# One burst of TensorE for a unit's y and the next unit's C.B and B^T x, with decays made in place

## Chip, cores, metric

The kernel runs on one core of a Trainium2 chip. The metric is device time in microseconds (us) of one execution. Engines are named as the profile names them: PE (TensorE), PEld (its weight loads), DVE (VectorE), ACT (ScalarE), POOL (GpSimd), SP (SyncE).

## The reference

```python
# x (4,8,768,32), a, B, C: 4 batches, 8 heads, 768 tokens, head 32, state 16
for c in range(seq // 32):                      # Mamba2 scan, by chunk
    cum = np.cumsum(log(clip(a)), -1)           # decays
    M = einsum(C, B) * causal(exp(cum_i - cum_j))
    y = einsum(M, x) + einsum(C, state) * exp(cum)
    state = exp(sum) * state + sum(B x * exp(cum_last - cum))
# then, for all 3072 tokens of width 256, in fp32
h = y @ w_in;  g = h * sigmoid(h);  out = g @ w_out      # 256 -> 2048 -> 256
```

## The kernel before

It works in 12 units of 256 tokens (four chunks of 64 tokens each). The scan of later units is slipped between the full matmuls of the two-layer part, which fill PE. One pair of units is one stage of eight slots; a slot is 14 full matmuls of 0.432 us (two passes each), 6.04 us. For each unit PE gets two bursts of small tiles. The first burst needs `BT`, a product that GpSimd makes of B and the decays:

```python
def f_B(u, engine=nc.gpsimd):
    BT[u] = sc.tile([128, 2, H, N], FP32, name="BT")
    engine.tensor_tensor(out=BT[u], in0=bn[u], in1=E[u][:, :, :, Q-1:Q]..., op=ALU.mult)

def f_G(u):
    f_D0(u)      # B^T x: 32 (24) tiles of 64 rows x 32 columns, needs BT[u]
    f_G0(u)      # C.B:   32 tiles of 32 x 64

def f_Y(u):      # [cut]
    # state part: 32 (24) tiles of 32 x 64, then
    # y inside the chunks: 64 tiles of 64 x 32, accumulated over it

def scan_plan(G):                      # [cut] which slot each piece stands in
    plan[j + 1][0].extend([E1[2], E1[3], partial(f_B, u), partial(f_C, u)])
    plan[j + 1][2].append(partial(f_G, u))
    ...
    plan[j + 2][2].append(partial(f_Y, u))
```

A plan's lists are emitted between the slot's seven matmul groups. GpSimd also adds output pieces (`p_add`, 128x256, four in a row in some slots). GpSimd runs its instructions in the order in which they were emitted.

## Time and profile before

| | before |
|---|---|
| median of 3 runs | 351.63 us (351.53 to 351.83) |
| profiled span | 350.1 us |
| PE busy | 343.5 us (98%) |
| granted clock, mean | 1.00 |

The prediction below shows the rows that carry the argument.

The timeline of POOL shows where BT stood: right at the start of its slot, 2.3 us ahead of the burst at 198.50, with a length of 0.64 us (columns: start, length, engine, line, operation, operands, idle time before).

```profile
196.20 0.64 POOL L340 TENSOR_TENSOR BT<-bn,E 128x256 f32<-128x256 f32 x1 [2.74 <-DVE E L303]
```

VectorE's timeline at the four additions of 203.73, which the prediction shows, has a pair of additions from SBUF (TN) beside the last of them:

```profile
206.20 1.82 DVE L534 TENSOR_TENSOR TN<-gT 128x512 f32<-128x512 f32 x2
```

And the chain of waits around unit 4's y (L458 and L467), with full matmuls in front of it and behind it and no hole:

```profile
91.68 1.73 PE hp L495 x8
93.41 0.62 PE gy L458 x32
94.03 0.79 PE gy L467 x53
94.82 1.92 PE o_ps L631 x8
```

### The profile page before, as it was taken

Reading aid. Unit: us, or ns where it says so; the run is one execution under the profiler, and the core shown is the slowest. Engines: PE = TensorE matmul, PEld = TensorE weight load, DVE = VectorE, ACT = ScalarE, POOL = GpSimd, SP = SyncE. Lnnn points to the kernel's source line nnn. Section 1 sums busy time; section 2 is a strip of 40 time slices with the busy share of each in tenths; the row PEclk is TensorE's granted clock in tenths of the full one; section 3 lists DMA queues with packets and bytes.
Section 4 is the critical chain, followed back from the end, with each engine's and each line's share of the span. In section 5 each row is a group of like instructions: output and inputs, shape, how many; then the busy total and the mean of one; then the engine's idle time right before and its main releaser. Section 6 shows DMA issues by size and latency. Waiting matters only on the chain.

```text
span 350.1 us, 8358 instructions
## 1 busy us (share of the span) xinstructions
PE 343.5 (98%) x3307; PEld 287.6 (82%) x3308; DVE 205.7 (59%) x408; ACT 162.3 (46%) x396; POOL 112.4 (32%) x140
## 2 busy tenths in 40 slices
PE   8989999999999999999999999999999999999996
PEld 3668888888888888888888888888888888888884
DVE  7998979976795764544663563664652231234812
ACT  2577585323323545355645454644545454454100
POOL 4445335443185032244042244042234112041200
PEclk9999999999999999999999999999999999999999
DMA  6978987799766789965179955057404237512202
GB/s 114 221 239 201 259 279 141 123 214 205 141 123 120 130 171 166 160 122 85 20 160 168 175 100 105 16 106 144 86 2 75 51 56 143 99 38 42 42 2 46
DMA packets 117376, 42.79 MB, mean 122 GB/s; under 512 B 102488, under 2 KB 109144, under 8 KB 117336
## 3 DMA queue, kind: packets, MB, share of 16 engines
q1 hardware_dynamic: 110328, 25.67, 34.9%
q0 software_dynamic: 4464, 16.25, 24.9%
q10 hardware_dynamic: 2544, 0.33, 0.6%
q8 instruction: 26, 0.43, 0.5%
q14 instruction: 14, 0.11, 0.1%
HBM read 22.83 MB, written 3.15 MB: 74 GB/s over the span
## 4 chain that ended last, share of the span: by engine, by line
PE 91%; DVE 4%; DMA 2%; issue 1%; SPq 0%; ACTq 0%; POOL 0%; ACT 0%; DVEq 0%
PE o_ps L631 36%; PE hp L686 28%; PE hp L495 15%; PE hp L631 3%; PE gy L467 2%; PE o_ps L617 2%; PE gy L404 2%; PE gy L458 2%; DMA gT<-in_a_dram 1%; PE gy L389 1%; DVE wv L178 1%; DVE E L415 1%; DMA tbc<-in_B_dram 1%; DVE st L430 0%; DMA out_dram<-ot 0%
## 5 line engine op out<-in xcount | busy, mean ns | idle before, releaser
L689 DVE TENSOR_TENSOR gT<-hp,p 128x256 f32<-128x256 f32 x64 | 26.9, 420 | 73.8 <-ACT p L700 37.8
L495 PE MATMUL hp<-XM,w_in_sb 128*128 128x256 f32 x256 | 59.4, 382 | 1.1 <-POOL w_in_sb L182 0.9
L631 PE MATMUL o_ps<-gT,w_out_sb 128*128 128x256 f32 x240 | 60.4, 379 | 0.0
L692 ACT ACTIVATE gT<-gT 128x256 f32<-128x256 f32 x96 | 39.7, 414 | 43.8 <-DVE gT L689 43.8
L495 PEld LDWEIGHTS hp<-XM,w_in_sb 128*128 128x128 f32 x256 | 47.8, 190 | 9.2 <-POOL w_in_sb L182 2.0
L686 PE MATMUL hp<-raw 128*128 128x256 f32 x192 | 52.7, 380 | 0.0
L548 POOL TENSOR_TENSOR ps<-ps 128x256 f32<-128x256 f32 x35 | 29.3, 838 | 71.4 <-ACT ps L578 70.1
L631 PEld LDWEIGHTS o_ps<-gT,w_out_sb 128*128 128x128 f32 x240 | 45.4, 190 | 6.3
L543 POOL DMA_DIRECT2D gT<-gT x31 | 27.2, 907 | 65.8 <-PE hp L686 22.9
L686 PEld LDWEIGHTS hp<-raw 128*128 128x128 f32 x192 | 36.2, 190 | 5.4 <-POOL ps L548 0.6
L700 ACT ACTIVATE p<-hp 128x256 f32<-128x256 f32 x64 | 24.6, 384 | 27.4 <-PE hp L686 25.9
L689 DVE TENSOR_TENSOR gT<-hp,u 128x256 f32<-128x256 f32 x32 | 13.6, 424 | 38.8 <-PE hp L686 38.8
L686 PE MATMUL hp<-XM,w_in_sb 128*128 128x256 f32 x128 | 34.1, 389 | 0.0
L497 ACT ACTIVATE gT<-hp 128x512 f32<-128x512 f32 x32 | 18.9, 595 | 27.3 <-PE hp L495 27.3
L686 PEld LDWEIGHTS hp<-XM,w_in_sb 128*128 128x128 f32 x128 | 23.3, 190 | 4.3 <-issue 1.0
L303 DVE TENSOR_TENSOR_SCAN E<-ab,diag 128x256 f32<-128x256 f32 (+1 forms) x32 | 25.3, 832 | 0.4
L578 ACT ACTIVATE ps<-o_ps 128x256 f32<-128x256 f32 x38 | 14.5, 383 | 23.9 <-PE o_ps L631 21.0
L340 POOL TENSOR_TENSOR BT<-bn,E 128x256 f32<-128x256 f32 x12 | 9.4, 782 | 47.8 <-DVE E L303 39.6
L631 PE MATMUL o_ps<-gT,wu 128*128 128x256 f32 x88 | 22.4, 380 | 0.0
L631 PE MATMUL o_ps<-gT,wv 128*128 128x256 f32 x88 | 22.2, 380 | 0.0
L631 PE MATMUL o_ps<-gT,raw 128*128 128x256 f32 x80 | 20.5, 380 | 0.0
L686 PE MATMUL hp<-raw,w_in_sb 128*128 128x256 f32 x64 | 19.1, 380 | 0.0
(125 smaller groups left out, 520.8 us busy)
## 6 DMA issues: line engine op xcount, KB each, us to landing
gT<-gT POOLq DMA_DIRECT2D x31, 512.0 KB, 6.1
ab<-in_a_dram SPq DMA_DIRECT2D x40, 128.0 KB, 3.2
raw<-in_moe_w_in_dram SPq DMA_DIRECT2D x8, 512.0 KB, 5.6
raw<-in_moe_w_out_dram SPq DMA_DIRECT2D x8, 512.0 KB, 6.0
xt<-in_x_dram SPq DMA_DIRECT2D x24, 128.0 KB, 5.3
out_dram<-ot SPq DMA_DIRECT2D x92, 32.0 KB, 1.7
bn<-in_B_dram SPq DMA_DIRECT2D x22, 64.0 KB, 2.4
tbc<-in_C_dram SPq DMA_DIRECT2D x40, 32.0 KB, 4.8
```

Source lines behind the costliest of these rows:

```text
L303: nc.vector.tensor_tensor_scan(out=E[u].rearrange("p k h t -> p (k h t)")[:, Q * g0:Q * (g0 + n)], data0=t.rearrange("p g t -> p (g t)"), ...
L340: engine.tensor_tensor(out=BT[u], in0=bn[u], in1=E[u][:, :, :, Q - 1:Q].to_broadcast([128, 2, H, N]), op=ALU.mult)
L495: nc.tensor.matmul(out=hp[:, i], lhsT=w_in_sb[:, kc, f * 128:(f + 1) * 128], rhs=xm[:, kc], start=(kc == 0), stop=(kc == KC - 1))
L497: nc.scalar.activation(GTS[g][:, :, j], hp, AF.Silu)
L543: nc.gpsimd.dma_start(out=o[:, js], in_=a[:, js], accum_op=ALU.add)
L548: engine.tensor_tensor(out=o, in0=p, in1=q, op=op)
L578: nc.scalar.activation(pn, on, AF.Copy)
L631: nc.tensor.matmul(out=o, lhsT=w(j), rhs=g()[:, j], start=(j == 0), stop=(j == last))
L686: nc.tensor.matmul(out=o, lhsT=w, rhs=x_, start=start, stop=True, skip_group_check=True)
L689: nc.vector.tensor_tensor(out=o, in0=p, in1=q, op=ALU.add)
L692: nc.scalar.activation(o, i, AF.Silu)
L700: nc.scalar.activation(o, i, AF.Copy)
```

## The change

The intent: PE pays for every change of tile mode (in the trace of the kernel before, 0.093 us behind a full pass and about 0.092 at the other changes), so y of unit u, C.B and B^T x of unit u+1 are put into one burst for u = 4 and 6 to 10; the state part of y becomes 16 (12) wide tiles. To have the next unit's decays in time they are made earlier, over their own input. The diff, cut to its core:

```diff
-    loads2 = ...(tc.tile_pool(name="loads2", bufs=2))
+    loads2 = ...(tc.tile_pool(name="loads2", bufs=3))
-            E[u] = sc.tile([128, 2, H, Q], FP32, name="E")
+            E[u] = ab[u] if u in ab else loads2.tile([128, 2, H, Q], FP32, name="ab")
+    gy = ps_s.tile([128, 4, 512], FP32, name="gy")     # one PSUM tile for all units
+    def f_Y0w(u):                                      # wide state part
+        ...
+                nc.tensor.matmul(out=yp[:, 2*w+c, 64*k:64*k+64], lhsT=sp[64*w:64*w+64, t],
+                                 rhs=cw[64*w:64*w+64, Q*t:Q*t+Q], start=False, stop=True, ...)
+    def f_YG(u):
+        f_G0(u + 1)
+        f_D0(u + 1)
+        f_Y1(u, True)
+        f_Y0w(u)
     [cut: scan_plan is rewritten]
+        decays(c, 3, 4, 4, 5)      # the last part, with f_B(c), stands in slot 5
+        burst(b, 5)                # f_YG(b), at the end of slot 5
```

More of the change, by code (lines that the diff above doesn't have):

```diff
@@ L59 @@
     loads = ctx.enter_context(tc.tile_pool(name="loads", bufs=3))
-    loads2 = ctx.enter_context(tc.tile_pool(name="loads2", bufs=2))
+    loads2 = ctx.enter_context(tc.tile_pool(name="loads2", bufs=3))
     rawp = ctx.enter_context(tc.tile_pool(name="rawp", bufs=7))
@@ L84, in load_pa @@
         b, t0 = at(u)
-        pa[u] = loads.tile([128, UT], FP32, name="pa")
+        pa[u] = sc2.tile([128, UT], FP32, name="pa")
         q.dma_start(out=pa[u], in_=bass.AP(tensor=a.tensor, offset=a.offset + b * H * S + t0,
@@ L263 @@
         nc.vector.tensor_reduce(out=par[:, e:e + 1], in_=hm[:, e::2], op=ALU.add, axis=AX.X)
+    par4 = const.tile([128, 4], FP32, name="par4")
+    nc.gpsimd.tensor_tensor(out=par4, in0=hm[:, 0:4], in1=hm[:, 4:8], op=ALU.add)
     pz = const.tile([128, 4, Q + 1], FP32, name="pz")
@@ L270 @@
             nc.gpsimd.memset(t[:, :, 0:1], n)
-    E, M, BT, BH, CT, CE, CW, PFX, ST, SM, DP, XM, GTS, BX = ({} for _ in range(14))
+    E, M, BT, BH, CT, CE, CW, PFX, ST, SM, XM, GTS, BX = ({} for _ in range(13))
+    gy = ps_s.tile([128, 4, 512], FP32, name="gy")
+    yp = gy[:, :, 384:512]
     def f_P01():
@@ L382, in f_D0 @@
         else:
-            DP[u] = ps_s.tile([128, 4, 512], FP32, name="gy")
-            d = [DP[u][:, c, 256:384] for c in range(2)]
+            d = [gy[:, c, 256:384] for c in range(2)]
         d = [o.rearrange("p (k x) -> p k x", k=2) for o in d]
@@ L397, in f_G0 @@
         bh, ce = BH.pop(u), CE[u]
-        if u not in DP:
-            DP[u] = ps_s.tile([128, 4, 512], FP32, name="gy")
         for k in range(2):
@@ L403, in f_G0 @@
                 for g in range(4):
-                    nc.tensor.matmul(out=DP[u][64 * c:64 * c + 64, g, 128 * k:128 * k + 128],
+                    nc.tensor.matmul(out=gy[64 * c:64 * c + 64, g, 128 * k:128 * k + 128],
                                      lhsT=bh[32 * g:32 * g + 32, ts], rhs=ce[32 * g:32 * g + 32, :, ts],
@@ L414, in f_M @@
         M[u] = m = E[u].rearrange("p k (g e) t -> p k g (e t)", e=2)
-        nc.vector.tensor_tensor(out=m[:, k], in0=DP[u][:, :, 128 * k:128 * k + 128], in1=m[:, k], op=ALU.mult)
+        nc.vector.tensor_tensor(out=m[:, k], in0=gy[:, :, 128 * k:128 * k + 128], in1=m[:, k], op=ALU.mult)
     def f_S(u, t0=0, t1=4):
@@ L431, in f_S, with f_SM, f_GMD, f_SMD @@
                                                in1=BX[u][c][:, k], op0=ALU.mult, op1=ALU.add)
-    def f_SM(u):
+    def f_SM(u, wide=False):
         t0 = 1 if u % UPB == 0 else 0
-        SM[u] = sc.tile([128, 4, 64], FP32, name="sm")
-        for e in range(2):
-            nc.scalar.activation(SM[u][:, t0:, 32 * e:32 * e + 32], ST[u][:, t0:, 32 * e:32 * e + 32],
-                                 AF.Copy, scale=par[:, e:e + 1])
-    def f_GMD(u):
+        SM[u] = sc.tile([128, 4, 128], FP32, name="sm")
+        for e in range(4 if wide else 2):
+            nc.scalar.activation(SM[u][:, t0:, 32 * e:32 * e + 32], ST[u][:, t0:, 32 * (e % 2):32 * (e % 2) + 32],
+                                 AF.Copy, scale=(par4 if wide else par)[:, e:e + 1])
+    def f_GMD(u, wide=False):
         f_G(u)
+        f_SMD(u, wide)
+    def f_SMD(u, wide=False):
         f_S(u)
-        f_SM(u)
+        f_SM(u, wide)
         for k in range(2):
             f_M(u, k)
-    def f_Y(u):
+    def f_Y0(u):
         first = u % UPB == 0
-        sp, cw, m, xc = SM.pop(u), CW.pop(u), M.pop(u), xt.pop(u)
-        m = m.rearrange("p k g (e t) -> p k (g e) t", e=2)
-        y = ps_s.tile([128, 4, 512], FP32, name="gy")
+        sp, cw = SM.pop(u), CW.pop(u)
         for t in range(1 if first else 0, 4):
@@ L457, in f_Y, with f_Y1 @@
                 w, q = divmod(g, 2)
-                nc.tensor.matmul(out=y[64 * q:64 * q + 64, 2 * w + c, 64 * k:64 * k + 64],
-                                 lhsT=sp[32 * g:32 * g + 32, t], rhs=cw[32 * g:32 * g + 32, Q * t:Q * t + Q],
+                nc.tensor.matmul(out=yp[64 * q:64 * q + 64, 2 * w + c, 64 * k:64 * k + 64],
+                                 lhsT=sp[32 * g:32 * g + 32, t, :64], rhs=cw[32 * g:32 * g + 32, Q * t:Q * t + Q],
                                  start=(k == 0 or (first and t == 2)), stop=False,
                                  tile_position=(32 * g, 64 * q), skip_group_check=True)
+    def f_Y0w(u):
+        sp, cw = SM.pop(u), CW.pop(u)
+        for t in range(1 if u % UPB == 0 else 0, 4):
+            k, c = divmod(t, 2)
+            for w in range(2):
+                nc.tensor.matmul(out=yp[:, 2 * w + c, 64 * k:64 * k + 64], lhsT=sp[64 * w:64 * w + 64, t],
+                                 rhs=cw[64 * w:64 * w + 64, Q * t:Q * t + Q], start=False, stop=True,
+                                 tile_position=(64 * w, 0), skip_group_check=True)
+    def f_Y1(u, start):
+        m, xc = M.pop(u), xt.pop(u)
+        m = m.rearrange("p k g (e t) -> p k (g e) t", e=2)
         for k in range(2):
@@ L466, in f_Y @@
                         h = 4 * w + q
-                        nc.tensor.matmul(out=y[32 * q:32 * q + 32, 2 * w + c, 64 * k:64 * k + 64],
+                        nc.tensor.matmul(out=yp[32 * q:32 * q + 32, 2 * w + c, 64 * k:64 * k + 64],
                                          lhsT=xc[64 * c:64 * c + 64, k, h], rhs=m[64 * c:64 * c + 64, k, h],
-                                         start=False, stop=True, tile_position=(64 * c, 32 * q),
+                                         start=start and k == 0, stop=not start, tile_position=(64 * c, 32 * q),
                                          skip_group_check=True)
-        DP[u] = y
+    def f_Y(u):
+        f_Y0(u)
+        f_Y1(u, False)
+    def f_YG(u):
[3 more added lines that the diff above has]
+        f_Y0w(u)
     def f_X(u):
         XM[u] = xmp.tile([128, 4, 128], FP32, name="XM")
-        y = DP.pop(u)
         n = 2 if u < 2 else 4
         for i in range(0, 4, n):
-            nc.scalar.activation(XM[u][:, i:i + n], y[:, i:i + n, 0:128], AF.Copy)
+            nc.scalar.activation(XM[u][:, i:i + n], yp[:, i:i + n], AF.Copy)
     def new_g():
@@ L713, in f_x1 @@
                 add(g0[:, 0, j], W, p1)
-                other(dve, 2 if j in (2, 5) else 0)
+                other(dve, 2 if len(dve) > 5 else 0)
             elif what == "5":
@@ L768, in scan_piece @@
             elif what == "G":
-                f_GMD(u)
+                f_GMD(u, u == 4)
+            elif what == "J":
+                f_YG(u - 1)
+                f_X(u - 1)
+                f_C(u)
+                f_SMD(u)
             elif what == "Y":
@@ L776, in scan_plan @@
         plan = [([], [], []) for _ in range(8)]
-        for i in range(2):
-            u, j = 2 * G + i, 3 * i
-            E0 = [partial(f_E0, u, q, 2) for q in range(2)]
-            E1 = [partial(f_E1, u, q, 4) for q in range(4)]
-            plan[j][0].extend([partial(f_P0, u), partial(f_P1, u), E0[0], E0[1], E1[0], E1[1]])
-            plan[j][1].extend([partial(f_T2, u, 0), partial(f_T2, u, 1)])
-            plan[j + 1][0].extend([E1[2], E1[3], partial(f_B, u), partial(f_C, u)])
-            plan[j + 1][2].append(partial(f_G, u))
-            plan[j + 2][0].extend([partial(f_S, u, 0, 2), partial(f_S, u, 2, 4), partial(f_M, u, 0),
-                                   partial(f_M, u, 1)])
-            plan[j + 2][1].append(partial(f_SM, u))
-            plan[j + 2][2].append(partial(f_Y, u))
-            plan[j + 3][1].append(partial(f_X, u))
-            if u + 1 < NU:
-                plan[(2, 7)[i]][0].extend([partial(f_T, u + 1, 0), partial(f_T, u + 1, 1)])
+        a, b, c = 2 * G, 2 * G + 1, 2 * G + 2
@@ new lines, in states, with decays @@
+        def states(u, j):
+            plan[j][0].extend([partial(f_C, u), partial(f_S, u, 0, 2), partial(f_S, u, 2, 4), partial(f_M, u, 0),
+                               partial(f_M, u, 1)])
+            plan[j + 1][1].append(partial(f_SM, u, u + 1 < NU))
+        def decays(u, *js):
+            todo = ([partial(f_P0, u), partial(f_P1, u), *(partial(f_E0, u, q, 2) for q in range(2))],
+                    [partial(f_E1, u, q, 4) for q in range(2)], [partial(f_T, u, i) for i in range(2)],
+                    [partial(f_E1, u, q, 4) for q in range(2, 4)] + [partial(f_B, u)])
+            for j, part in zip(js, todo):
+                if 0 <= j < 8:
+                    plan[j][0].extend(part)
+            if js[3] < 8:
+                plan[js[3]][1].extend([partial(f_T2, u, 0), partial(f_T2, u, 1)])
@@ new lines, in burst @@
+        def burst(u, j):
+            plan[j][2].append(partial(f_YG if u + 1 < NU else f_Y, u))
+            plan[j + 1][1].append(partial(f_X, u))
+        if G == 3:
+            plan[0][0].extend([partial(f_E1, a, 2, 4), partial(f_E1, a, 3, 4), partial(f_B, a)])
+            plan[0][1].extend([partial(f_T2, a, 0), partial(f_T2, a, 1)])
+            plan[0][2].append(partial(f_G, a))
+            states(a, 1)
+            decays(b, 1, 1, 2, 2)
+            burst(a, 2)
+            states(b, 3)
+            decays(c, 4, 4, 5, 5)
+        else:
+            decays(b, -1, 0, 0, 1)
+            burst(a, 1)
+            states(b, 2)
+            if c < NU:
+                decays(c, 3, 4, 4, 5)
@@ L792, in scan_plan @@
+        burst(b, 5)
+        if c < NU:
+            states(c, 6)
+            decays(c + 1, 7, 8, 8, 9)
         return plan
@@ L905 @@
             f_s2(2)
-        scan_piece(4, j, ("TE", "DCS", "G", "YS", "", "", "", ""))
-        scan_piece(5, j, ("", "", "T", "E", "DCS", "G", "YS", ""))
+        scan_piece(4, j, ("TE", "DCS", "G", "S", "", "", "", ""))
+        scan_piece(5, j, ("", "", "T", "E", "DS", "J", "YS", ""))
         scan_piece(6, j, ("",) * 7 + ("t",))
@@ L911 @@
                 f_XT(2, i)
+            f_P(6)
+            for q in range(2):
+                f_E0(6, q, 2)
+            for q in range(2):
+                f_E1(6, q, 4)
         f_s2((4, 4, 4, 4, 4, 2, 0, 4)[j])
@@ L920 @@
             f_TS(1, 3, 0)
-        if j in (2, 5):
-            load_unit(6 + j // 3)
+        if j in (2, 5, 7):
+            load_unit({2: 6, 5: 7, 7: 8}[j])
+    NEXT = {(2, 2): 9, (2, 5): 10, (3, 1): 11}
     for G in range(2, NU // 2):
@@ L944 @@
                     f_XT(G + 1, i)
-            if j in (2, 5) and 2 * G + 4 + j // 3 < NU:
-                load_unit(2 * G + 4 + j // 3)
+            if (G, j) in NEXT:
+                load_unit(NEXT[G, j])
     P = NU // 2 - 1
```

## The prediction

Four readings of the kernel before (timeline of PE and PEld, 177 to 187 us) belong beside the text. What it calls a drain is the gap that the records show at a change of mode: the last full pass starts at 177.278 and the first small one at 177.588, which is 0.093 us more than the usual 0.216. Its 0.054 us for 64 columns is a quarter of that 0.216; waves of B^T x, which have 64 columns, start 0.055 us apart there. Where it takes 0.107 us for 128 columns, of a pass or of a load, the trace shows 0.109 for both. That some passes of y go slower than others is measured (0.238 and 0.376 us for 32 each); why is not shown, and that y goes at the slower rate behind 32 other pairs was my estimate.

> **What bounds the kernel now.** I read the page first: busy shares, the forty slices, the chain that ended last.
>
> ```profile
> PE 343.5 (98%) x3307; PEld 287.6 (82%) x3308; DVE 205.7 (59%) x408; ACT 162.3 (46%) x396; POOL 112.4 (32%) x140
> ...
> PE   8989999999999999999999999999999999999996
> ...
> DVE  7998979976795764544663563664652231234812
> ...
> PE 91%; DVE 4%; DMA 2%; issue 1%; SPq 0%; ACTq 0%; POOL 0%; ACT 0%; DVEq 0%
> ```
>
> TensorE (PE) is full from slice 5 to the last but one, and 91% of the chain is PE. A busy PE need not be at its peak, so I next read the chain of waits in order of time over one stage. Its columns are start, length, what:
>
> ```profile
> 177.23 0.43 PE o_ps L631 x2
> 177.66 0.36 PE gy L389 x24
> 178.01 0.62 PE gy L404 x32
> 178.64 1.06 PE hp L686 x4
> 179.70 0.86 PE o_ps L631 x4
> ...
> 184.45 0.43 PE o_ps L631 x2
> 184.88 0.62 PE gy L458 x32
> 185.50 0.79 PE gy L467 x53
> 186.29 1.06 PE hp L686 x4
> 187.35 1.29 PE o_ps L631 x6
> ```
>
> A full 128x128 matmul of 256 columns takes 0.216 us (0.86 for four), one after the other, without a hole. L389 is B^T x, L404 is C.B, L458 and L467 are the two halves of y: small tiles that stand between the full ones. So each unit of the scan costs PE two bursts. B^T x with C.B costs 178.64 - 177.66 = 0.98 us, plus 1.06 - 0.86 = 0.20 for the slow first full matmul behind it: 1.18 us (24 passes of B^T x; 1.20 with 32). y costs 186.29 - 184.88 + 0.20 = 1.61 us (1.49 where the first part has 24 passes). Everything else here runs beside PE. A change is worth what it takes from these bursts, less any wait that it puts in front of PE.
>
> [...] By the start of each pass in the records, the first small pass comes 0.093 us late behind a full one, and B^T x to C.B, the two halves of y, and the way back each show about 0.092 us beyond the columns still streaming (0.054 us for 64 columns, 0.107 for 128). [...] behind a drain two full loads start 0.109 us apart, and the first wave of a mode loses 0.104 us with 128 columns of weights, 0.050 with 64, 0.025 with 32. [...] in y's second part the first 32 passes go in 0.238 us, the next 32 take 0.376.
>
> **The change, part by part.** (a) C.B and B^T x of unit u+1 now stand with y of unit u in one burst, for u = 4, 6, 7, 8, 9, 10: six merged bursts, with 4's and 6's C.B and 5's and 11's y still alone. (b) In the merged burst the order is C.B, B^T x, the intra-chunk part of y, then the state part, which becomes 8 matmuls of 64 rows x 128 columns (16 passes, or 12) in place of 32 (24) of 32x64. (c) The scan E is written over its own input; decays start about four slots earlier. (d) ScalarE makes four masked state slices instead of two. (e) The order of PSUM and buffers follows.
>
> Cost of a merged burst from the durations above: entry 0.093; C.B 0.425 from first to last start; to B^T x 0.197; B^T x 0.238; the y part has the same 64x32 mode, so no drain, but it now comes behind 32 pairs[...], so I charge it all at the slower rate: 0.67; to the state part 0.146; the state part; way back 0.146 + 0.104. The state part decides. It has 64 moving columns (0.054 us), but each load has 128 columns (0.107 us). Two row tiles run side by side, so 8 waves x 0.107 = 0.856 us, against 0.477 for the 32 narrow passes before[...]. With 12 passes it is 0.64.
> Sum, 32 and 16 passes: 0.093 + 0.425 + 0.197 + 0.238 + 0.67 + 0.146 + 0.856 + 0.250 = 2.88 us. With 24 passes of B^T x 2.81[...]. With 32 and 12, 2.66.
> Before: the same pairs cost 1.18 + 1.61 = 2.79, 1.20 + 1.61 = 2.81 and 1.20 + 1.49 = 2.69.
> Six bursts after: 3 x 2.81 + 2.88 + 2 x 2.66 = 16.63 us. Before: 3 x 2.79 + 2.81 + 2 x 2.69 = 16.56. So what is saved by two fewer mode changes (about 0.3 us each burst) goes back into wide weight loads. Net about 0[...].
>
> New waits. A merged burst needs the next unit's BT (POOL, L340) about 0.7 us after it starts. At slot 5 of the first two scan stages that plan for units 8 and 10, the built order puts BT on POOL behind four additions of the outputs. Where those stand, timeline of POOL:
>
> ```profile
> 203.73 3.15 POOL L548 TENSOR_TENSOR ps<-ps 128x256 f32<-128x256 f32 x4 [6.25 <-ACT ps L578]
> ```
>
> The slot's matmuls begin at 199.61 and end 14 x 0.432 = 6.04 us later. The additions end at 206.88, slot + 7.27; BT takes 0.64, so it is ready at slot + 7.9 and a semaphore later. B^T x wants it at 6.04 + 0.093 + 0.425 + 0.197 = 6.76. PE waits 1.18 us, twice: 2.4 us. Before, BT stood in slot 4, where POOL had only its buffer copies ahead: at 196.19 it ran 2.3 us ahead of the burst at 198.5.
> In the stage that plans unit 7, VectorE gets eleven items in one slot: states 1.1, masks 2 x 0.64, prefix 0.98, clipping 1.0, two scans 1.26, besides three additions of 0.42. That is about 6.9 us for a slot of 6.04, and TN's 0.65 behind it, so an addition that a following matmul accumulates over comes about 0.3 us late; I take 0.4 us in all.
> Sum: 0.07 + 2.36 + 0.4 = 2.8 us[...]: +2.4.
>
> (c) by itself wins nothing: in the waits of the kernel before, PE waits for no scan from 45 us on, and at the start the scan of unit 1 stands on VectorE behind the weights' bit work (the chain has L178 at 15.23, then L303 at 16.45), not behind y. (d) adds 2 x 0.31 us of ScalarE per unit, which is busy about half of the time.
>
> **Rivals.**
> 1. The wide loads are hidden and the state part streams at 0.055 us per wave: 8 x 0.055 = 0.44 instead of 0.86. Then each burst saves 0.42 more, 2.4 us over six (12 passes save less), and the total is 351.7 with the waits, or about 349 without. For it: the narrow loads do overlap matmuls. Against it: they overlap one load per matmul, and here the load is the longer of the two.
> 2. The two row tiles do not load side by side: 16 x 0.107 = 1.7 us, +0.86 a burst, +4.6 us in all: about 358.5. Against it: before, four row tiles load in one wave of 0.058 us.
> 3. No wait for BT, because the drain and C.B in front cover it: 351.5 and below. Against: the POOL sum above misses by over a microsecond.
> 4. VectorE becomes the bound in the crowded slots and PE waits in each: 357 or more. Its row in the forty slices shows 4 to 7 tenths there, so only the one stage is at risk.
>
> **Range and chances.** Predicted 354.0 us (351.63 + 2.4). Low end 350.8: rival 1 with most of the waits[...]. High end 356.6: waits in three bursts and costlier decays. 2% is 7.0 us, more than all twenty bursts of units 2 to 11 could give by halving mode changes, so faster by 2% has 0.02; slower by 2% needs rival 2 or 4 with the waits: 0.05; within 2%: 0.93.
>
> **What would show each step.** The time from the last full matmul before a merged burst to the second after it: 2.7 to 2.9 us where there is no wait. The starts of the 16 wide passes: pairs 0.107 us apart (mine), 0.055 (rival 1), or singly 0.107 (rival 2). The 64 passes of y: 0.67 us or about 0.45. In the waits, a PE load of B^T x waiting for POOL BT, twice, 1.0 to 1.3 us each, in slot 5 before the bursts that hold units 8's and 10's B^T x; if it is absent, the step on POOL's order is wrong. In the stage of units 6 and 7, PE waits for VectorE's additions of some tenths. The last stage without scan (281.5 to 321.8 us before) should keep its 40.3 us. I am wrong if merged bursts cost 2.4 us or less with no wait in front, or if the state part is slower than loads side by side allow.

## More of the kernel before

The clock row, granted clock in tenths for 40 slices, says that PE was never slowed:

```profile
PEclk9999999999999999999999999999999999999999
```

## The result

The changed kernel takes 365.33 us (363.39 to 366.22, six runs) against 351.64 (351.48 to 352.05, six runs of the kernel before). The ratio is 1.0384, with an interval of 1.0357 to 1.041: slower by 3.8%, outside the predicted range of 350.8 to 356.6. All ratios here are the mean time of one kernel's fast runs over that of the other's of the same rounds, so they are not quite the ratio of the medians. All runs count as fast except where said.

The page of the changed kernel: span, busy times, the PE and clock rows, and the shares of the chain that ended last.

```profile
span 363.2 us, 8181 instructions
...
PE 348.5 (96%) x3219; PEld 293.7 (81%) x3220; DVE 209.6 (58%) x408; ACT 165.5 (46%) x408; POOL 114.4 (31%) x141
...
PE   7989999999899999979999979999999999999996
...
PEclk9999999999999999969999998999999999999999
...
PE 85%; DVE 5%; POOL 2%; issue 2%; DMA 2%; ACT 1%; SPq 0%; ACTq 0%; DVEq 0%; POOLq 0%
```

PE has 88 instructions fewer and is still busy 5.0 us longer. Busy time that grows with less work points to a slower clock, and the clock row has two dents, in slices 18 and 25. PE's row has a 7 in slice 18 and one in slice 24, just before the second dent. The waits of PE name what stands there (engine, line, what it waited for: us in total, times, longest):

```profile
PE gy L394 <- POOL BT L346: 4.7, 2, 2.6
PE o_ps L660 <- ACT ps L607: 1.3, 1, 1.3
```

The chain of waits through the first dent. The stretch of 0.74 us called issue is the last of four additions in a row on POOL, which the chain does not name:

```profile
152.14 0.73 POOL ps L577
...
152.94 1.22 POOL ps L577
...
154.23 0.99 POOL ps L577
...
155.57 0.74 issue
156.31 1.09 POOL BT L346
...
157.45 0.43 PE gy L394 x24
157.88 0.99 PE gy L487 x58
158.87 1.90 PE gy L474 x16
160.77 2.00 PE hp L715 x4
```

BT stands behind four output additions, as predicted, but it ends at 157.39, B^T x starts 0.05 us behind that, and PE waits 2.67 us. Then the wide state part (L474) takes 1.90 us and four passes of a full matmul take 2.00 us. A merged burst without a wait has the same parts at their true size:

```profile
187.14 0.62 PE gy L407 x32
187.76 0.39 PE gy L394 x32
188.15 0.71 PE gy L487 x40
188.86 1.04 PE gy L474 x16
189.90 1.06 PE hp L715 x4
```

So behind the wait PE ran at half speed. The windows show it; each row is a stretch, its length, each engine's busy time with the number of instructions, and then the granted clock, the DMA share and GB/s:

```profile
151.02:154.43 3.41, 3.41 (x32) 2.67 (x38) 1.82 (x3) 2.73 (x8) 2.13 (x3) 1.00 0.38 71
154.43:157.84 3.41, 0.81 (x70) 0.57 (x57) 2.47 (x4) 0.42 (x1) 3.33 (x4) 1.00 0.57 101
157.84:161.26 3.42, 3.42 (x85) 3.07 (x72) 0.00 (x0) 0.00 (x0) 0.76 (x2) 0.50 1.03 204
161.26:164.67 3.41, 3.41 (x9) 2.70 (x8) 0.89 (x3) 0.48 (x2) 0.28 (x1) 0.50 0.89 135
215.87:219.28 3.41, 1.41 (x102) 1.32 (x102) 1.45 (x2) 0.17 (x1) 2.77 (x3) 1.00 0.08 17
219.28:222.69 3.41, 3.41 (x18) 2.84 (x15) 0.00 (x0) 0.38 (x1) 0.67 (x1) 0.50 0.78 147
```

Both kernels run the same 1376 passes of full matmuls (128x128, 256 columns) in the same order, so the start of each, counted by its number, says where the one falls behind the other. The last of them is 13.25 us late:

| where | us | how it was read |
|---|---|---|
| start and unit 3 | +0.2 | before 80 us |
| six merged bursts by themselves | +0.6 | 17.18 in place of 16.56 |
| waits for BT at 154, 215 and 133 us | +5.05 | 2.67 + 2.19 + 0.19 |
| half clock behind the first two | +4.7 | 2.1 inside the bursts, 2.6 in full matmuls |
| wait for ScalarE at 94.9 | +1.45 | the hole that y of unit 4 had filled |
| pause at 191.2, called issue | +0.9 | also in experiment 6's profile; left open |
| small waits for VectorE | +0.3 | at 115, 132 and 176 us |

These make 13.2. The hole at 94.9 is new, and the chain shows it, ended by ScalarE's copies of C (L371) and the eviction behind them:

```profile
93.69 0.91 ACT ce L371 x2
94.60 0.28 ACT ps L607
...
94.92 1.99 PE o_ps L660 x8
```

In the kernel before, unit 4's y ran from 93.41 to 94.82, so PE was at work while ScalarE caught up, and the burst cost nothing. The change takes it away there and pays for it 7 us later.

### The profile page after: what moved, and what is told of

Its sections match the earlier page's. It is cut to its first block, busy times and chain, and to the rows that moved or that the text cites.

```text
span 363.2 us, 8181 instructions
## 1 busy us (share of the span) xinstructions
PE 348.5 (96%) x3219; PEld 293.7 (81%) x3220; DVE 209.6 (58%) x408; ACT 165.5 (46%) x408; POOL 114.4 (31%) x141
## 3 DMA queue, kind: packets, MB, share of 16 engines
HBM read 22.83 MB, written 3.15 MB: 72 GB/s over the span
## 4 chain that ended last, share of the span: by engine, by line
PE 85%; DVE 5%; POOL 2%; issue 2%; DMA 2%; ACT 1%; SPq 0%; ACTq 0%; DVEq 0%; POOLq 0%
PE o_ps L660 32%; PE hp L715 25%; PE hp L524 15%; PE hp L660 3%; PE gy L487 2%; PE o_ps L646 2%; PE gy L474 2%; POOL ps L577 1%; PE gy L407 1%; DVE ab L418 1%; DMA tbc<-in_B_dram 1%; PE gy L394 1%; DVE st L433 1%; DVE ab L309 1%; PE gy L463 1%
## 5 line engine op out<-in xcount | busy, mean ns | idle before, releaser
L660 PE MATMUL o_ps<-gT,w_out_sb 128*128 128x256 f32 x240 | 61.3, 383 | 2.0 <-ACT ps L607 1.3
L524 PE MATMUL hp<-XM,w_in_sb 128*128 128x256 f32 x256 | 59.4, 382 | 1.0 <-POOL w_in_sb L182 0.6
L577 POOL TENSOR_TENSOR ps<-ps 128x256 f32<-128x256 f32 x35 | 30.6, 875 | 91.9 <-ACT ps L607 90.6
L524 PEld LDWEIGHTS hp<-XM,w_in_sb 128*128 128x128 f32 x256 | 47.8, 190 | 9.0 <-POOL w_in_sb L182 2.0
L715 PE MATMUL hp<-XM,w_in_sb 128*128 128x256 f32 x128 | 35.5, 401 | 0.0
L715 PEld LDWEIGHTS hp<-XM,w_in_sb 128*128 128x128 f32 x128 | 24.7, 198 | 3.9 <-issue 0.2
L309 DVE TENSOR_TENSOR_SCAN ab<-ab,diag 128x256 f32<-128x256 f32 (+1 forms) x32 | 26.7, 874 | 0.3
L346 POOL TENSOR_TENSOR BT<-bn,ab 128x256 f32<-128x256 f32 x12 | 10.0, 831 | 35.2 <-DVE ab L309 30.2
```

Source lines behind the costliest of these rows:

```text
L309: nc.vector.tensor_tensor_scan(out=E[u].rearrange("p k h t -> p (k h t)")[:, Q * g0:Q * (g0 + n)], data0=t.rearrange("p g t -> p (g t)"), ...
L524: nc.tensor.matmul(out=hp[:, i], lhsT=w_in_sb[:, kc, f * 128:(f + 1) * 128], rhs=xm[:, kc], start=(kc == 0), stop=(kc == KC - 1))
L577: engine.tensor_tensor(out=o, in0=p, in1=q, op=op)
L660: nc.tensor.matmul(out=o, lhsT=w(j), rhs=g()[:, j], start=(j == 0), stop=(j == last))
L715: nc.tensor.matmul(out=o, lhsT=w, rhs=x_, start=start, stop=True, skip_group_check=True)
```

## The experiments

My theory after the result: the merged burst by itself is worth about nothing, and the loss is BT's lateness plus a half clock which that wait brings about. Rivals: the merged burst itself (its small tiles, its wide loads) lowers the clock; the in-place decays cost the time; the four additions are slow whatever VectorE does.

### 1. BT on VectorE

```diff
-  ... + [partial(f_B, u)])
+  ... + [partial(f_B, u, nc.vector)])          # the changed kernel, units 7 to 11
```

> The changed kernel with B times its decay (BT) computed on VectorE instead of GpSimd for units 7 to 11, nothing else. My theory: in the changed kernel PE waits for BT behind GpSimd's four output additions (2.67, 2.19 and 0.19 us beyond the usual 0.197 between C.B and B^T x), and the waits of over 2 us pull TensorE's granted clock to half for 6.8 and 3.4 us, which costs about 4.5 us more. Then here the waits go, the clock stays at 1.00, and the time is 365.3 - 5.0 - 4.5 = 355.8 us (355 to 357). Rival: the clock falls because the small tiles themselves count as low activity; then it still falls twice and the time is about 360.

Measured: 357.38 us (355.63 to 357.65), ratio 1.0142 (1.0115 to 1.0169), 0.4 above the theory's range and well under the rival's 360. No wait for POOL's BT is left, and the clock is 1.00 through all six merged bursts, which cost 2.73 to 2.96 us where they do not wait. So merged bursts alone do not lower the clock. The rest over the kernel before is, beside the bursts themselves, mainly in two places: the hole at 94.9, unchanged, and a new wait. (BT is still 0.77 us late once, now from VectorE, at the burst near 155 us.) It shows in the waits between 174 and 187 us:

```profile
DVE ot L583 <- DMA out_dram<-ot: 2.6, 1, 2.6
PE hp L715 <- DVE gT L718: 1.8, 1, 1.8
```

VectorE stands at an output transpose whose buffer waits for an output transfer, and PE waits for the addition behind it. In the three kernels with BT on VectorE (experiments 1 to 3) PE loses 2.0 us or more here; of all others only experiment 10's loses anything here, 0.6 us. So a lateness that was taken from one engine came back on another.

### 2 and 3. Narrow state part, and an order by mode

Both are built on experiment 1. Each has a small ordering read on VectorE (`touch`) in the burst, between parts that write PSUM in different pieces.

```diff
 f_G0(u + 1); +touch(); f_D0(u + 1); f_Y1(u, True); -f_Y0w(u) +f_Y0(u, True)      # 2
-f_G0(u + 1); f_D0(u + 1); f_Y1(u, True); f_Y0w(u)
+f_Y0(u); touch(); f_Y1(u, False); f_D0(u + 1); f_G0(u + 1)                       # 3
```

> As e1_bt_vec, with the state part of the merged burst as 32 (or 24) narrow passes of 32x64 tiles instead of 16 (12) wide ones of 64x128; a tiny read on VectorE orders it behind C.B[...]. If the wide passes are bound by loading 128 columns of weights, the last part falls from 0.837 to about 0.48 us and the way back from 0.201 to 0.146, less about 0.15 us of waiting for the tiny read: -0.25 us a burst, -1.5 us over six: 354.3. Rival, the last part costs its drain and not its loads: no shorter, and the time is e1's or 0.5 us more.

> As e1_bt_vec, with the merged burst ordered by tiling mode: state part narrow (32x64), then y's intra part and B^T x (64x32), then C.B (32x64); again a tiny read on VectorE. Sum of parts: 0.093 + 0.477 + 0.146 + 0.15 (read) + 0.64 + 0.27 + 0.146 + 0.425 + 0.197 + 0.104 = 2.65 us a burst instead of 2.9: 354.3 us, and no wait for BT even were it late, since B^T x comes third. Rival, that a merged burst is slowed by its mere length[...]: 2.9 us or more as in e1.

Measured: 361.15 us (ratio 1.0252, 1.0226 to 1.0277) and 359.85 us (1.0179, 1.0111 to 1.0248). The profiled run of the second is slow, so I read from it only lengths inside a burst. The narrow state part takes 0.477 us from first to last start (0.360 with 24 tiles), the wide one 0.837 (0.614 with 12). In the changed kernel the two wide passes of a pair start 0.007 us apart, the pairs 0.112, and so do the pairs of their loads, where a wave of 64 columns takes 0.055 in B^T x: I read this as the wide loads binding, as predicted. But the ordering read costs 0.35 to 0.39 us (my guess was 0.15) in each burst that nothing else delays (1.2 in unit 4's, which I did not explain), so such bursts come to 2.82 and 2.87 us in experiment 2 and 2.78 to 2.83 in experiment 3. PE's wait behind the output transfer grows to 4.0 us in experiment 2, with 3.41 us of half clock behind it. The slow profile of experiment 3 has the same (2.9 and 3.41 us), which is not counted here; its fast runs have mean clocks of 0.995, 0.995 and 1.000. Both theories said 354.3 us: as a way to gain, both failed.

### 4. A long wait in the kernel before

```diff
-        engine.tensor_tensor(out=BT[u], ...)
+        for _ in range(9 if u == 9 else 1):           # the kernel before
+            engine.tensor_tensor(out=BT[u], ...)
```

> The kernel BEFORE, with the GpSimd multiplication for unit 9's BT done nine times over (same result), so that PE waits once, in front of B^T x of unit 9, about 3 us (4.8 us more on GpSimd, 1.7 us of it slack). No merged burst in it. If a wait of that length halves the granted clock, it falls to half behind this one wait for one or two stretches of 3.4 us, and the time is 351.6 + 3.1 + 1.7 to 3.4 = 356.4 to 358. If the clock fell for another reason in the changed kernel, it stays at 1.00 here and the time is 354.7.

Measured: 358.46 us (ratio 1.0183, 1.0161 to 1.0205). There is no merged burst here, only one wait:

```profile
PE gy L390 <- POOL BT L341: 4.0, 1, 4.0
```

```profile
198.33:201.74 3.41, 0.34 (x2) 0.00 (x0) 0.42 (x1) 0.74 (x2) 3.02 (x6) 1.00 0.41 99
201.74:205.15 3.41, 2.43 (x66) 1.84 (x67) 0.00 (x0) 0.00 (x0) 1.48 (x3) 0.50 0.47 78
205.15:208.57 3.42, 3.42 (x10) 2.70 (x9) 1.52 (x6) 0.38 (x1) 0.00 (x0) 0.50 0.57 114
```

By the start of each full matmul the kernel loses 6.94 us: 4.12 of wait, and 2.8 of half clock. A wait alone brings the low clock about.

### 5. The in-place decays alone

```diff
-    loads2 ... bufs=2        +    loads2 ... bufs=3            # the kernel before
-    pa from loads            +    pa from sc2
-    E[u] = sc.tile(...)      +    E[u] = ab[u] if u in ab else loads2.tile(...)
```

> The kernel before with one part of the change alone: the decays E are made in place of a, whose ring has three buffers, and pa comes from another pool; no burst is merged and nothing moves in the schedule. Theory (the loss is in the merged bursts and in what they wait for): 351.6 us, within 0.4 of the kernel before, clock 1.00 throughout, no wait of TensorE for BT. Rival (the in-place decays and the longer hold of the a buffers cost time themselves): 353 us or more, with loads or ScalarE's exponentials in a new wait.

Measured: 353.35 us (352.88 to 354.63, four runs; before 351.99), ratio 1.003 (0.9986 to 1.0073). It is 1.7 us over my figure and falls in the rival's range of 353 or more, but the interval contains 1. In the profiled run, the fastest of the four (352.88), 0.6 us is lost before 26 us, where the weights are made, and nothing afterwards; in front of this loss stand PE's waits of 0.3 us for ScalarE and 0.7 us called issue, which the kernel before does not have. That matches the loss of 0.4 us at the start of the changed kernel. By the interval this part may cost up to 2.6 us; it is not the cause of a loss of 13.7.

### 6. VectorE's additions one slot later

```diff
-            if j == 5:        # the changed kernel
+            if j == 6:
                 f_T1(G, 0); f_T1(G, 1); f_TS(G, 3, 0)
```

> The changed kernel with one move: the two triangle additions and the scan step of VectorE that stood in slot 5 stand in slot 6, so that they no longer run beside the four output additions of GpSimd that BT is queued behind. Theory (these additions took 0.99 to 1.25 us in place of 0.73, and BT 1.08 in place of 0.64, because VectorE worked in SBUF at the same time): the four additions go back to 0.72 to 0.8 us each and BT to 0.64 to 0.8; the wait at the burst near 215 us falls from 2.19 us to between 1.0 and 1.5, that near 154 us from 2.67 to 1.5 to 2.2; the clock no longer falls behind at least the second of them; 359 to 363 us. Rival (the additions are long by themselves or for PSUM, and only a later start of them counts): both waits stay within 0.3 us of what they were, the clock falls twice, 365 us.

Measured: 362.10 us (360.02 to 363.88), ratio 1.027 (1.0217 to 1.0323). This run tells why the waits were twice my figure. At the second late burst, POOL in the changed kernel and in this one:

```profile
213.11 3.66 POOL L577 TENSOR_TENSOR ps<-ps 128x256 f32<-128x256 f32 x4 [11.45 <-ACT ps L607]
216.74 1.08 POOL L346 TENSOR_TENSOR BT<-bn,ab 128x256 f32<-128x256 f32 x1
```

```profile
210.15 3.13 POOL L577 TENSOR_TENSOR ps<-ps 128x256 f32<-128x256 f32 x4 [11.66 <-ACT ps L607]
213.24 0.64 POOL L346 TENSOR_TENSOR BT<-bn,ab 128x256 f32<-128x256 f32 x1
```

In the changed kernel VectorE runs these beside them (first row), and this pair stands in the same place at the first late burst (second row, of the experiment, where it could not be moved):

```profile
215.51 1.81 DVE L563 TENSOR_TENSOR TN<-gT 128x512 f32<-128x512 f32 x2
```

```profile
153.51 1.75 DVE L309 TENSOR_TENSOR_SCAN ab<-ab,diag 128x256 f32<-128x256 f32 x2
```

With VectorE's additions gone, four output additions take 3.13 us and BT 0.64, close to the 3.15 and 0.64 that the prediction used, and PE waits 1.21 us: the predicted 1.18. At the first burst the second and third addition still take 1.21 and 0.99 us beside the two scans, the fourth and BT fall from 1.05 and 1.08 to 0.72 and 0.64, and the wait falls from 2.67 to 1.89. VectorE's additions of one SBUF and one PSUM tile (gT from hp), which also run there, lengthen nothing: an addition of POOL beside them takes 0.73. Scans and TN additions have two SBUF inputs, and where they and POOL's additions or BT overlap in the changed kernel, each instruction but the first ends 0.5 to 0.6 us after the other engine's has ended, as if it had had to wait for that. At the second burst the ends are TN 216.19, addition 216.77, TN 217.32, BT 217.82. So an addition goes from 0.72 to as much as 1.26, a scan from 0.68 to 1.15 and a TN addition from 0.68 to 1.21.

The profiled run has no half clock at these bursts. Of the four runs two have a mean clock of 0.998 or more (360.02 and 361.20 us) and two 0.991 (362.99 and 363.88). A mean clock does not say where it was lost, so that the same waits cost half clock in some executions and not in others is an inference.

### 7. A short wait in the kernel before

As experiment 4, with five in place of nine.

> The kernel before with GpSimd's B^T product for unit 9 computed five times in place of once, so that one burst of TensorE waits. A dose: eight extra products gave a wait of 4.12 us and a half clock of 6.83 us; four are an estimate of 1.5 us. Theory (a wait of about 1.5 us is too short to halve the clock, one of 2 to 3 us may, by where it falls): the time grows by the wait alone, 353.1 us (+1.5, within 0.4), clock 1.00 in every record. Rival (any wait over 1 us halves the clock): the wait of 1.5 and a half clock of at least 3.4 us, 354.8 us or more, mean clock 0.995 or less.

Measured: 353.42 us (353.19 to 353.60), ratio 1.0026 (0.9984 to 1.0067; two outlying runs of the kernel before, 354.40 and 355.41, widen intervals). The profile shows one wait at that burst, 1.25 us beyond the usual start, and no loss behind it (0.4 us more is lost before 104 us, far in front of it):

```profile
197.66:201.07 3.41, 2.23 (x71) 1.57 (x69) 0.42 (x1) 0.95 (x3) 2.87 (x5) 1.00 0.94 193
```

The median is 1.4 over the kernel before, close to the wait alone. This wait cost itself and nothing more.

### 8. A repaired change

```diff
 f_YG:   f_Y0(u); f_Y1(u, False); f_D0(u + 1); touch(); f_G0(u + 1, (3, 0, 1, 2))
-        decays(c, 3, 4, 4, 5)      +        decays(c, 3, 3, 4, 4)
 units 4 and 5 in separate bursts; state part narrow; opool bufs=3
```

> A repaired change: units 4 and 5 keep their separate bursts, those of 6 to 10 are merged in the order state part (narrow, 32x64), y inside the chunks, B^T x, C.B, so that the tile mode changes only three times; C.B alone waits for a small VectorE read of the last y; the last decays of a unit are made one slot earlier, so that BT stands ahead of the four output additions on GpSimd; the output tiles have three buffers. Theory (a burst itself is saved only by fewer mode changes and narrow loads, and the loss of the changed kernel was BT's wait, its half clock and VectorE's order): each merged burst 2.4 to 2.6 us against a pair of 2.79 before, no wait over 1 us, clock 1.00, 349.8 to 351.6 us, so 0.995 to 1.000 of before. Rival (merging always pays for itself elsewhere, because a hole that the separate burst filled for free stays open and a new wait of VectorE's strict order stands at the burst): 352.5 to 357 us, with waits for VectorE or ScalarE of 0.5 us or more at three or more of the five bursts.

Measured: 356.23 us (355.97 to 359.68, six runs), ratio 1.0135 (1.0087 to 1.0183). My theory's figure fell here. The rival's figure came, but not its sign: behind 50 us PE waits for VectorE or ScalarE by 0.5 us or more only twice (2.1 and 0.6 us). BT is never waited for, the hole at 94.9 is gone (no full matmul between 79 and 119 us loses more than 0.04 us against the kernel before), but each merged burst still costs 2.78 to 3.01 us: B^T x hides only part of the ordering read, and the gap before C.B is 0.47 to 0.61 us in place of 0.146. And VectorE waited for a load of the decays' input, and PE for VectorE, 2.1 us. I put this down to the decays being made a slot earlier, but experiment 9, where they are not, has the same wait; its cause stays open.

```profile
DVE ab L327 <- DMA ab<-in_a_dram: 2.2, 2, 1.7
```

```profile
PE hp L721 <- DVE gT L724: 2.7, 2, 2.1
```

### 9. Units 4 and 5 back to separate bursts

```diff
-  4: ("TE", "DCS", "G", "S", ...)      5: (..., "E", "DS", "J", "YS", "")
+  4: ("TE", "DCS", "G", "YS", ...)     5: (..., "E", "DCS", "G", "YS", "")
```

> The changed kernel with units 4 and 5 back to two separate bursts each, as before; units 6 to 10 stay merged. Theory (merging unit 4's y cost 1.45 us at 94.9 us, because the y burst had stood there in a hole in which TensorE waits for ScalarE anyway, and 0.14 us in the burst itself): 363.7 us, 1.6 us less than the changed kernel, the wait of 1.3 us for ScalarE's ps gone, the two waits for BT and the low clock as they were, 0.985. Rival (the wait for ScalarE is a loss of the in-place decays or of the moved loads and not of the merging): the wait of 1.3 us stays, 365.3 us within 0.5.

Measured: 363.06 us (362.10 to 367.37), ratio 1.0322 (1.025 to 1.0395). The wait of 1.3 us for ScalarE is gone, and the full matmuls between unit 4's y and the burst at 115 us gain 2.0 us in all on the changed kernel. The rival falls: merging unit 4 opened the hole. In the profiled run this is given back by a wait of 2.1 us near 131 for VectorE, which waits for a load of the same tensor as in experiment 8. BT's two waits are the same, 2.67 and 2.19 us, but this time only the first is followed by half clock:

```profile
213.69:217.10 3.41, 2.49 (x41) 1.69 (x39) 1.93 (x4) 2.09 (x6) 3.17 (x4) 1.00 0.02 5
217.10:220.52 3.42, 2.22 (x109) 2.05 (x110) 0.65 (x1) 0.00 (x0) 2.10 (x4) 1.00 0.30 57
220.52:223.93 3.41, 3.41 (x17) 3.01 (x16) 0.89 (x3) 1.93 (x5) 0.55 (x1) 1.00 0.54 101
```

Why the same wait costs different amounts can be read from the records of the clock. In each profile every spell of half clock starts a whole number of 3.413 us steps from every other, 3.413 us being the length of the shorter spell in the changed kernel (the longer is 6.827). They start there at 157.84, 219.28 and, after the work, 362.64, which is 18 and 60 steps from the first; in experiment 4 at 201.74 and 355.34, 45 steps. I infer from this that the clock is decided in windows on a fixed grid; in every window shown here the granted clock is 0.50 or 1.00. The rows above are cut on each run's own grid. Here the wait (215.9 to 218.1) straddles the border at 217.10: neither window falls under 2.22 us of busy PE, and the clock stays. In the changed kernel a wait as long fell almost whole into one window, which left 1.41 us busy, and the clock was halved. In all profiles together, up to the end of PE's work, the six windows at full clock with 0.34 to 1.41 us busy (0.81 and 1.41 in the changed kernel, 1.24 and 0.34 in experiments 2 and 4, 0.51 in the slow profile of experiment 3, and one in experiment 9) were each followed by half clock. The lowest that was not had 1.48, in experiment 8:

```profile
130.46:133.87 3.41, 1.48 (x6) 1.06 (x6) 3.41 (x8) 2.43 (x7) 1.61 (x2) 1.00 0.59 118
```

The sixth run of the changed kernel itself, 363.39 us at a mean clock of 0.991 where the others have 0.981 to 0.986, fits a run in which the second spell did not come; it has no profile, so this is an inference.

### 10. BT wanted last, and VectorE's additions later

Experiment 9 with the move of experiment 6 and with B^T x at the end of the merged burst:

```diff
 f_YG:   f_G0(u + 1); -f_D0(u + 1); f_Y1(u, True); f_Y0w(u); +f_D0(u + 1)
```

> The last kernel with two moves more: B^T x stands last in each merged burst (C.B, y, wide state part, B^T x), so that BT is needed some 1.8 us later, and VectorE's two triangle additions stand one slot later. Theory (after the unit 4 hole, the loss is BT's lateness and the half clock that follows it): waits of 1.89 and 1.21 us fall to 0.1 and 0, the clock is 1.00, each of five bursts costs an estimate of 3.0 us for one mode change more against 2.79 of a pair, which is +1.05, and with 0.5 of start and 0.2 of small VectorE waits the kernel takes 353.0 to 354.3 us. Rival (the late BT only moves to the next wait, because VectorE's states and the M product come later by as much): waits for VectorE or ScalarE of 1 us or more at two or more later bursts, 356 us or more.

Measured: 356.40 us (354.47 to 357.64, six runs), ratio 1.0114 (1.0069 to 1.0158). BT is waited for nowhere, and outside the start PE's longest wait for another engine from 50 us on is 0.4:

```profile
PE hp L715 <- DVE gT L718: 0.4, 1, 0.4
```

The clock is full to the end. The burst sum was right: 2.81, 3.07, 3.03, 2.81 and 3.00 us, 0.95 over the pairs of the kernel before (expected 1.05). The whole is still 2 us over my figure. In the profiled run 1.5 us is lost at the start, before 27 us, against 0.5 that I took, and some 1.8 us in small waits, against 0.2. The rival's later waits of 1 us did not come. This version gives back some two thirds of the loss and shows what merging in this order is worth without waits: less than nothing, by one microsecond of bursts. No version here beat the kernel before.

## Why the prediction was wrong

- **The bound, and the burst's own cost.** Right to within 0.1 us a burst. PE was the bound, and six bursts gave +0.6 us where I had +0.07. The terms that were small: the way back behind wide tiles is 0.201 us and not 0.146 (0.33 over six bursts), and from B^T x to y there is a gap of 0.024 to 0.036 that I had left out. y inside the burst took 0.64 to 0.69 us (predicted 0.67), the wide part 0.837 and 0.614 (0.856 and 0.64). Rivals 1, 2 and 3 fell. Rival 4's figure (357 or more) came, but not on its road: PE's waits for VectorE are 0.3 us in all. (The sum's last line goes from 2.8 to +2.4. It takes 0.3 off for the chance that y is not slowed, an estimate of mine, and has a slip, 2.8 less 0.3 being 2.5; it changes nothing.)
- **The wait for BT: mechanism right, size wrong.** The mis-sized term of the sum is "The additions end at 206.88, slot + 7.27; BT takes 0.64". I took both durations as if they were fixed, each from a place where GpSimd was not held up. In the kernel before, a pair of TN additions stood beside the last addition too (206.20, shown above). But there the fourth addition began 0.06 us before the pair (206.14), kept its 0.73, and VectorE was late (1.22 for the first TN); and BT did not stand behind it. In the changed kernel TN began 0.007 us before the addition at 215.52, and the addition took 1.26. The page before already warned: its means are 838 ns for these additions and 782 for BT, not 0.72 and 0.64 us. In the changed plan the additions stand beside two scans, then TN, or beside TN: 3.15 became 4.21 and 3.66, 0.64 became 1.08. 1.18 with these differences gives 1.18 + 1.06 + 0.44 = 2.68 and 1.18 + 0.51 + 0.44 = 2.13; measured 2.67 and 2.19. Experiment 6 took VectorE's work away and got 1.21.
- **The missing step.** The sum has no term for what a wait does to the clock: +4.7 us, nearly as much as the waits themselves. At 1.18 us, as predicted, it would most likely have been zero: a wait of 1.25 us cost no clock in experiment 7, nor did one of 1.21 in the profile of experiment 6. So the error in the durations took the waits from harmless to harmful, and was paid twice.
- **Pairs were not all worth their length.** "So each unit of the scan costs PE two bursts" counts every burst of the kernel before as cost. Unit 4's y stood in a hole that ScalarE sets anyway, and taking it away saved nothing there: 1.45 us, which experiment 9 gave back.
- **VectorE's crowded slot and the decays in place.** About right: 0.3 to 0.5 us of small waits near units 6 and 7 (predicted 0.4), and the decays gain nothing. That they cost some 0.6 us at the start was not in it.
- **The end.** No full matmul from 267 us on loses anything, as predicted.

Left open: the pause of 0.9 us at 191.2, which experiment 6's profile has behind the same burst (0.9 us at 188.2) and no other has; why a spell of half clock lasts one window behind the wait at 215 us (3.41 us) and two behind that at 154 us (6.83 us, although PE was busy for all 3.42 us of the first); what makes the start up to 1.5 us later in the kernels with in-place decays.

## What to carry to other kernels

Before moving work earlier or merging it, list for each operand who makes it, behind what in that engine's order, and beside what on the other engine, where GpSimd and VectorE work in SBUF at the same time (here an addition of GpSimd went from 0.72 us to as much as 1.26 that way); take durations from a stretch with the same neighbours and the same order of starts. Ask of a wait of the matmul engine how much of one clock window it leaves busy: here windows of 3.41 us with 1.41 us or less busy were followed by 3.4 or 6.8 us at half rate, and windows with 1.48 or more were not, so a wait of 2.19 us cost itself alone in one profile and 1.6 us more in another. And look at what a burst stands in: one that fills a hole, as unit 4's y did here (1.45 us), is free, and removing it is no gain.
